# A gated linear attention block and an MLP on one core: the order of the turns is searched anew

## The chip, the core and the metric

The kernel runs on one core of a Trainium2 chip. A core has a matrix engine (TensorE, PE in the profile, its weight loads PEld), three engines for elementwise work (VectorE or DVE, ScalarE or ACT, GpSimd or POOL) and SyncE (SP), which here only issues DMAs. Each engine works through its own queue of instructions in the order in which the program wrote them, and waits on semaphores for the others. The metric is the device time of one launch in microseconds; lower is better.

## The reference, cut to what matters

There are 4 batches, 8 heads, 768 positions and a head width of 48. The first half is a recurrence over time, the second a layer norm and an MLP with a residual. All tokens are float32; the two weight matrices come as float64.

```python
for t in range(S):                      # state: B, H, 48, 48
    state = alpha[:, :, t, :, None] * state + einsum('bhd,bhe->bhde', k[:, :, t], v[:, :, t])
    y[:, :, t] = einsum('bhd,bhde->bhe', q[:, :, t], state)
x  = y, heads side by side              # B, 768, 384
xn = (x - mean(x)) / sqrt(var(x) + 1e-6) * g_ln
out = x + maximum(xn @ w_ch1, 0) @ w_ch2     # 384 -> 1536 -> 384
```

## The kernel before

**Tiles.** The 768 positions are cut into 6 chunks of 128. A tile is one chunk of one batch, so there are 24 tiles; tile "c b" is chunk c of batch b. `attention(c, b)` does one tile. It sums log alpha with a triangular matrix, scales q and k with the exponentials, forms the masked products inside the chunk, adds the part that the state of the chunk before brings, and brings the state forward. It then normalises the row and puts it, transposed, into `xT`.

**One tile is 23 turns**, each up to a `yield`: `la` (ACT, L246); `lps` (PE, L249); `ek`, `eq` (ACT, L253 and L254); `qk` for k (POOL, L256); `qk` for q (DVE, L258); loads for a later tile (SP); the first transposes `tps` (PE, L272) and their copy `qkT` (ACT, L276); the second ones and their copy (ACT in chunks 0 and 1, DVE at L278 later); `aps` (PE, L285); two masked copies `at` (DVE, L289); a DMA; `yps` (PE, L302 and L307); `x` (ACT, L311); a DMA; `sps` (PE, L321); `st` (DVE, two adds, L326); `st` times the gate (POOL, L331); `stats` (DVE L335 and L336, ACT L338 and L339); `xn` (DVE, L342); `xps` (PE, L349); `xT` (ACT, L351).

**The MLP.** Chunk 0 is plain: 12 blocks `hidden` (PE L372, then a relu on ACT) and `project` (PE L384, a DVE add). Chunks 1 to 5 use fast matrix multiplication with fewer products. The first layer has two rounds r of 15 products, `hidden_product` (PE L612), each followed by a combining step on DVE or ACT and, in places, on POOL (L620 to L655). Its operands are sums of `xT` that `combine_x` makes on DVE (L588). The second layer has 20 products, `product` (PE L455), followed by DVE, ACT or POOL steps (L465 to L515). Its operands are sums of the hidden block that `combine_hidden` makes on DVE (L442), after `relus` (ACT L664).

**Weights.** `take_weights(i)` turns one of 12 pieces of 768 KB from float64 into float32: three DVE steps (L168, L170, L172), one ACT step (L174), then DVE again (L176 and three times L183 for the first matrix, or L179 for the second), then the load of piece i + 3 into one of three staging buffers, of which the one that was freed first is taken.

**PSUM.** Three pools limit how far TensorE can run ahead: tag "a", 3 buffers, for `lps`, `tps` and `aps` (which takes 2); tag "s", 2 buffers, for `yps`, `sps` and `xps`; tag "m", 3 buffers, for the products of the MLP.

**The order.** All these generators are advanced one turn at a time by the string `ORDER` (L25 to L44), read by the two lines at L694 and L695. A small letter a to x is tile number 4c + b (a is tile 0 0, e is tile 1 0, x is tile 5 3). A to L are the 12 pieces of weights. M is the MLP, one half product per letter: a turn of matrix products, then its combining step. X is `combine_x`, N `combine_hidden`, R `relus`, S the sums of weights (POOL), O the reload of x for the residual. As the engines' queues keep the order of the program, the string fixes every queue. Positions in it are counted from 0 below.

Of the kernel before, what the change touches and what calls it, by code (L numbers as in the profile page):

```python
# [22 lines left out]


ORDER = (  # L25
    "babdabcdcabadcbacabbdabaabacababdabacbdbccbadAccdddcBcCedfeacbacaeBeffcgbaededbe"
    "eghfbAefgfcachfbdcheaaffbaefgdjBddeedbdcgfbeicCjgdfihcgjdCeAhccAgBDfghddEfeOgegi"
    "DfDeeiMfhMMMiMDMMiegMGEgEMMMOfeGghhigMMjhiCEfggFMhOGFHFgMGghMiHkfMMfiHeFIjhfHeMM"
    "IkJSIhhkhhlMMjIMfMglKJKjJLfgMljjLKLhhMSSMihSikMhOSgiMMSSMgShjkSjhiiMXjiSXSiXiXMk"
    "kMXkSllMXMXMlSMMXnMnMMkSMSMSiXmMSXMnMSMSMSMSjkMMkikjMXlMMMMMMRMllMMMljOMRSMMMSlk"  # L30
    "jlklMjjSRimMMnMSMjRMMMnMMMMkMnnmnMMMkMRMpjMMMnMRlMlllnmMmiRmOlMSmMRmMoMmmOMMJMRM"
    "SmSjmNSjlRMMRmoNinjkkNMmNMMkolMNRpoMlOKpMNMmMMMoMmoNmMNkNMMMNMMNMnMNqMkMNMMMopMM"
    "NSMMnolMoMlNpkNMoMMMOkOMMonnXXXXpMMXXMMXXXpoMMMMMMMMpXMMXMMoMMMrMMMMqMMMrMMMmnMM"
    "pRMomRnprmmMRqRopMMpMRMoMMmRmMMMMMrprnMnrnMMMoopppnMtpMqRMMMOMtrqMqnMMoMpqMprMRq"
    "RMMqNsMqMOMNRMNtrRnrMNMqMqqNMssRMMMNssoMMMNMNNMNsMMMNopMqqqqqrMMNMMsNtpMMNMMOprM"
    "MMNqsMqtMMooMMsNpMMXMMsMXXMstMqrrXtuXXXMtMMXXMMvMMMMXsvMMMtXMstMOrMMMMMMMMMvMMrr"
    "rsMtMvOsMMrtMMMMLuRMsMMvvMMMMMRRMtMrRMuMORvxMMMRRMstrMMstRqttsMqRuMsMMNRMuMRNMMN"
    "NMvMtuurvMxMMMMNsNtRtMMwNNvMMMsrMNMwMMNNMNMMwtNMMuMMuuMMMMMNuMwMNMMNwMMuttsxMMuv"
    "XXXvxMvuuXXXXxvwxMXMxxMMuwMXMwxMMXMMXMMMMMvMMwMwMxMMMRMuOwMuOMMwMMMMwuMMxwMwRMRM"
    "MxRMMRMvMMMMwxMMMMMMMMMuMMuMRMRRvMMMRNwxuRMMvMOMRxMMxvwMMNwMxNNMNxRNMMuxMMwMNMvM"  # L40
    "MONMwMNNMNMMMNwMMNMxMxMMvMMxwNMONMMNxMMMvMMXvOXXXMXXXMMMMMMXXMMMMMMMMXMMMMMRMXMM"
    "RMMMMMMMMMMMMMMMRRMMMMORMMMMMRMMMMRMMMMMMMMMRMRRMRMMNMMMNMMMNNNRMMNNMNMNMMMNNMMM"
    "ONMNMMMMMMMMMMMMMNNMMNMMMMMMM"
)  # L44


# [678 lines left out]
```

## Time and profile before

| | |
|---|---|
| Time, median of 3 | 476.33 us (474.06 to 476.4) |
| Span of the profiled execution | 472.3 us, granted clock 1.000 |
| PE, PEld busy | 457.1 us (97%), 384.5 us (81%) |
| DVE, POOL, ACT busy | 356.6 (76%), 222.7 (47%), 152.9 us (32%) |
| HBM read and written | 33.20 MB and 9.48 MB, 90 GB/s over the span |

The profile is one execution. Its busy times are sums over an engine's instructions, with overlaps counted once. A matmul's record lasts longer than the distance to the next one, since matmuls are pipelined, so how well TensorE is used is read from the distances between the starts of its records. An engine's idle time is put down to the instruction or DMA that ended it.

### The profile page before, as it was taken

To read this page: it belongs to the slowest core of one execution; us is meant where nothing else is said; L and a number is where in the kernel's file an instruction comes from. 1 tells how busy PE (TensorE), PEld (TensorE's weight loads), DVE (VectorE), ACT (ScalarE), POOL (GpSimd) and SP (SyncE) were. 2 spreads that over 40 slices of the span, in tenths; PEclk is the share of its full clock that TensorE was granted. 3 is DMA by queue.
4 is the path that set the end of the run, shared out by engine and by line. 5 is a ranking of instruction groups with operands and counts; after the bars stand their busy time and mean duration, and the time that the engine had idled before them with its cause. 6 is when DMAs were issued, how large, how long until landed. Compare 5 with 4: busy or idle time off the path is not lost.

```text
span 472.3 us, 9365 instructions
## 1 busy us (share of the span) xinstructions
PE 457.1 (97%) x3690; PEld 384.5 (81%) x3690; DVE 356.6 (76%) x662; ACT 152.9 (32%) x335; POOL 222.7 (47%) x222
## 2 busy tenths in 40 slices
PE   7899999999999999999999999999999999998996
PEld 5768465567688889998898998898998899987896
DVE  3799899867377799876788867688677579765673
ACT  4576354511033523124342121543031341223300
POOL 4142103069969990727461426460435360544513
PEclk9999999999999999999999999999999999999999
DMA  8986856403301422240331231330020110210001
GB/s 260 334 248 196 282 157 224 123 19 102 85 17 52 129 75 67 70 118 15 104 101 52 86 102 51 83 101 1 34 81 23 35 35 0 80 56 0 1 18 51
DMA packets 40132, 43.29 MB, mean 92 GB/s; under 512 B 13956, under 2 KB 36228, under 8 KB 40088
## 3 DMA queue, kind: packets, MB, share of 16 engines
q1 hardware_dynamic: 39544, 42.56, 29.4%
q8 instruction: 29, 0.48, 0.4%
q10 hardware_dynamic: 544, 0.13, 0.1%
q14 instruction: 15, 0.12, 0.1%
HBM read 33.20 MB, written 9.48 MB: 90 GB/s over the span
## 4 chain that ended last, share of the span: by engine, by line
PE 85%; DVE 5%; POOL 4%; ACT 2%; DMA 2%; issue 2%; POOLq 0%; DVEq 0%; ACTq 0%
PE ops L455 24%; PE hps L612 24%; PE hps L372 7%; PE ops L384 7%; PE aps L285 5%; PE yps L307 4%; PE tps L272 4%; PE yps L302 4%; PE lps L249 3%; PE sps L321 2%; PE xps L349 2%; DMA rk<-in_k_dram 1%; DVE at L289 1%; DVE sum L588 1%; DMA ra<-in_alpha_dram 1%
## 5 line engine op out<-in xcount | busy, mean ns | idle before, releaser
L471 POOL TENSOR_TENSOR ob<-ob,u 128x192 f32<-128x192 f32 x40 | 27.5, 699 | 83.3 <-DVE ob L468 63.9
L612 PE MATMUL hps<-sum,w 128*128 128x256 f32 x240 | 59.9, 382 | 1.1 <-DVE hT L655 1.1
L612 PEld LDWEIGHTS hps<-sum,w 128*128 128x128 f32 x240 | 44.7, 190 | 7.9 <-DVE hT L655 1.5
L455 PE MATMUL ops<-w,hT 128*128 128x192 f32 x280 | 49.6, 328 | 0.0
L664 ACT ACTIVATE hT<-hT 128x512 f32<-128x512 f32 x60 | 36.3, 628 | 35.6 <-POOL hT L634 21.3
L455 PEld LDWEIGHTS ops<-w,hT 128*128 128x128 f32 x280 | 45.7, 190 | 1.1
L331 POOL TENSOR_TENSOR st<-st,gate 128x384 f32<-128x384 f32 x20 | 19.1, 959 | 53.6 <-DVE st L326 44.3
L631 POOL TENSOR_TENSOR hT<-hT,u 128x512 f32<-128x512 f32 x10 | 12.9, 1287 | 56.9 <-DVE u L630 56.9
L256 POOL TENSOR_TENSOR qk<-rk,ek 128x384 f32<-128x384 f32 x22 | 23.3, 1059 | 30.0 <-PE sps L321 12.6
L307 PE MATMUL yps<-rv,at 128*64 128x48 f32 x768 | 36.5, 219 | 0.1
L289 DVE COPY_PREDICATED at<-consts,aps 128x512 f32<-128x512 int32 x48 | 32.2, 724 | 3.6 <-PE aps L285 3.2
L307 PEld LDWEIGHTS yps<-rv,at 128*64 128x64 f32 x768 | 32.9, 138 | 0.6 <-DVE at L289 0.3
L372 PE MATMUL hps<-xT,w 128*128 128x512 f32 x72 | 32.4, 597 | 0.0
L384 PE MATMUL ops<-w,hT 128*128 128x384 f32 x96 | 32.2, 488 | 0.0
L612 PE MATMUL hps<-xT,w 128*128 128x256 f32 x120 | 31.1, 382 | 0.9 <-DVE hT L644 0.9
L285 PE MATMUL aps<-qkT 48*128 48x128 f32 x384 | 28.6, 285 | 2.1 <-DVE at L289 1.3
L285 PEld LDWEIGHTS aps<-qkT 48*128 48x128 f32 x384 | 23.8, 187 | 8.0 <-issue 4.0
L302 PE MATMUL yps<-st,qkT 112*64 112x96 f32 x320 | 29.8, 257 | 0.0
L455 PE MATMUL ops<-ws,sum 128*128 128x192 f32 x160 | 28.9, 328 | 0.7 <-DVE sum L442 0.7
L455 PE MATMUL ops<-ws,hT 128*128 128x192 f32 x160 | 29.5, 327 | 0.0
L276 ACT COPY qkT<-tps 112x512 f32<-112x512 f32 x32 | 18.2, 597 | 29.0 <-PE tps L272 25.7
L455 PEld LDWEIGHTS ops<-ws,sum 128*128 128x128 f32 x160 | 26.3, 190 | 1.4 <-DVE sum L442 1.0
(141 smaller groups left out, 1020.9 us busy)
## 6 DMA issues: line engine op xcount, KB each, us to landing
ws<-in_moe_w_ch_dram SPq DMA_DIRECT2D x12, 768.0 KB, 6.1
ra<-in_alpha_dram SPq DMA_DIRECT2D x24, 192.0 KB, 2.6
rk<-in_k_dram SPq DMA_DIRECT2D x24, 192.0 KB, 3.4
rq<-in_q_dram SPq DMA_DIRECT2D x24, 192.0 KB
rv<-in_v_dram SPq DMA_DIRECT2D x24, 192.0 KB, 2.8
kept<-x SPq DMA_DIRECT2D x24, 192.0 KB, 1.9
ob<-kept SPq DMA_DIRECT2D x24, 192.0 KB, 2.9
out_dram<-ob SPq DMA_DIRECT2D x19, 192.0 KB, 1.9
```

Of the source, the lines that this page charges most:

```text
L256: nc.gpsimd.tensor_mul(qk[:, 1, :, :D], raws.pop(("k", c, b)), ek)
L285: nc.tensor.matmul(aps[i][:, p], qkT[rows, 1, p], qkT[rows, 0, p], start=True, stop=True)
L289: nc.vector.copy_predicated(out=at[:, i], data=aps[i], mask=mask.unsqueeze(1).broadcast_to([P, NP, P]))
L302: nc.tensor.matmul(yps[s, p].rearrange("p a b -> p (a b)"), qkT[:, 0, p, s], sts[b][:R, p].rearrange("p a b -> p (a b)"), start=True, stop ...
L307: nc.tensor.matmul(yps[s, p, i], at[:, i, p, s], vt[:, 2 * p + i], start=(c == 0), stop=(c == 0 or i == 1))
L331: nc.gpsimd.tensor_mul(st, st, gate.unsqueeze(2).broadcast_to([P, NP, 2 * D]))
L372: nc.tensor.matmul(hps, w1[:, f, j * P:(j + 1) * P], xT_of[c][:, f], start=(f == 0), stop=(f == NF - 1))
L384: nc.tensor.matmul(ops_of[b], hT_of[c][:, j, b], w2[:, j], start=(j == 0), stop=(j == NJ - 1))
L455: nc.tensor.matmul(acc, lhs[:, j], rhs[:, j], start=(j == 0), stop=(j == NT - 1))
L471: getattr(nc.gpsimd, f"tensor_{op}")(x, x, y)
L612: nc.tensor.matmul(acc[:, i], w, b, start=True, stop=True)
L664: nc.scalar.activation(out=x, in_=x, func=AFT.Relu)
```

## The change

The string `ORDER` is replaced by another one with the same letters in the same numbers, 1389 turns. So every instruction, every buffer and every operand stays; what changes is the sequence in which each engine's queue holds them, and with it the buffer that is taken where a pool has several. The new string begins with tile 0 0 and carries it, and then tile 0 2 and tile 0 1, several steps forward at once, where the old one brings all four batches forward side by side; tiles of chunk 1 (e to h) come in between those of chunk 0, from position 45 on (55 before). The purpose is a shorter wait of the engines for each other.

```diff
 ORDER = (
-    "babdabcdcabadcbacabbdabaabacababdabacbdbccbadAccdddcBcCedfeacbacaeBeffcgbaededbe"
-    "eghfbAefgfcachfbdcheaaffbaefgdjBddeedbdcgfbeicCjgdfihcgjdCeAhccAgBDfghddEfeOgegi"
-    "DfDeeiMfhMMMiMDMMiegMGEgEMMMOfeGghhigMMjhiCEfggFMhOGFHFgMGghMiHkfMMfiHeFIjhfHeMM"
-    "IkJSIhhkhhlMMjIMfMglKJKjJLfgMljjLKLhhMSSMihSikMhOSgiMMSSMgShjkSjhiiMXjiSXSiXiXMk"
...
-    "MxRMMRMvMMMMwxMMMMMMMMMuMMuMRMRRvMMMRNwxuRMMvMOMRxMMxvwMMNwMxNNMNxRNMMuxMMwMNMvM"
-    "MONMwMNNMNMMMNwMMNMxMxMMvMMxwNMONMMNxMMMvMMXvOXXXMXXXMMMMMMXXMMMMMMMMXMMMMMRMXMM"
-    "RMMMMMMMMMMMMMMMRRMMMMORMMMMMRMMMMRMMMMMMMMMRMRRMRMMNMMMNMMMNNNRMMNNMNMNMMMNNMMM"
-    "ONMNMMMMMMMMMMMMMNNMMNMMMMMMM"
+    "aacaaacbbcbacaaaaccccbbccaadabbbbbddbbddbaaaaeaacaccdddbbbbAgddebeeggeecaddcfccc"
+    "eeeeaaffbebccfihgedddddffghhiibdfdbbdgffcdfeejefACcfdAAcdggggeeeffBBeeggOghhBfMk"
+    "MMMiiOhjjChhhhDDOlMMMMCMMDCkFFDGBEGfggfjgEhhMMFFeEEffiijiiiMgkkGhhhhIIggkgiieMMM"
+    "MIjjeiIjjjigMSShHjjkmffSiSSMMMkhGJJJgigllMMkkjkMHjjjHjjkkiLLihHKSSSKKMlOMMMLllnn"
...
+    "RRMsMMMrNNNMMRMMMwwNNNMMMNNNMMtMMMMtrMMMNNNNOMMMsMNMMvMMtNsMMttMMMMNMMMxxuMMMMvv"
+    "vXXXXXXXXwwwuvvvuuuMMMMuuuXXXMMMuxxxMMMMMMMMMMMMMMMwwwwwMMMMMMMMMRwMMRRRMRMMOMwM"
...
+    "vMMMNwwMwMOMMMMMMNMNNNNMMwMMMMMMMwxxMMvwMXvvXXXXXXMMMMMMXXXMMXMMMMMMMMMMMMMMMMMM"
+    "MRMMMMMMMMMMMMMMMMMMMMMMMMMMMMMRMRRRRRROOMMMMRRMMMMMNRNNMMMNNOMMRMMNNNMMMLNMMMNN"
+    "MMOMMMNNMMMNNNMMMMMMMMMMMMMMM"
 )
```

More of the change, by code (lines that the diff above doesn't have):

```diff
@@ L25 @@
 ORDER = (
-    "babdabcdcabadcbacabbdabaabacababdabacbdbccbadAccdddcBcCedfeacbacaeBeffcgbaededbe"
-    "eghfbAefgfcachfbdcheaaffbaefgdjBddeedbdcgfbeicCjgdfihcgjdCeAhccAgBDfghddEfeOgegi"
-    "DfDeeiMfhMMMiMDMMiegMGEgEMMMOfeGghhigMMjhiCEfggFMhOGFHFgMGghMiHkfMMfiHeFIjhfHeMM"
-    "IkJSIhhkhhlMMjIMfMglKJKjJLfgMljjLKLhhMSSMihSikMhOSgiMMSSMgShjkSjhiiMXjiSXSiXiXMk"
-    "kMXkSllMXMXMlSMMXnMnMMkSMSMSiXmMSXMnMSMSMSMSjkMMkikjMXlMMMMMMRMllMMMljOMRSMMMSlk"
-    "jlklMjjSRimMMnMSMjRMMMnMMMMkMnnmnMMMkMRMpjMMMnMRlMlllnmMmiRmOlMSmMRmMoMmmOMMJMRM"
@@ L32 @@
[L32 to L37, printed above, removed]
@@ L38 @@
-    "NMvMtuurvMxMMMMNsNtRtMMwNNvMMMsrMNMwMMNNMNMMwtNMMuMMuuMMMMMNuMwMNMMNwMMuttsxMMuv"
-    "XXXvxMvuuXXXXxvwxMXMxxMMuwMXMwxMMXMMXMMMMMvMMwMwMxMMMRMuOwMuOMMwMMMMwuMMxwMwRMRM"
-    "MxRMMRMvMMMMwxMMMMMMMMMuMMuMRMRRvMMMRNwxuRMMvMOMRxMMxvwMMNwMxNNMNxRNMMuxMMwMNMvM"
-    "MONMwMNNMNMMMNwMMNMxMxMMvMMxwNMONMMNxMMMvMMXvOXXXMXXXMMMMMMXXMMMMMMMMXMMMMMRMXMM"
-    "RMMMMMMMMMMMMMMMRRMMMMORMMMMMRMMMMRMMMMMMMMMRMRRMRMMNMMMNMMMNNNRMMNNMNMNMMMNNMMM"
-    "ONMNMMMMMMMMMMMMMNNMMNMMMMMMM"
+    "aacaaacbbcbacaaaaccccbbccaadabbbbbddbbddbaaaaeaacaccdddbbbbAgddebeeggeecaddcfccc"
@@ new lines @@
+    "eeeeaaffbebccfihgedddddffghhiibdfdbbdgffcdfeejefACcfdAAcdggggeeeffBBeeggOghhBfMk"
+    "MMMiiOhjjChhhhDDOlMMMMCMMDCkFFDGBEGfggfjgEhhMMFFeEEffiijiiiMgkkGhhhhIIggkgiieMMM"
+    "MIjjeiIjjjigMSShHjjkmffSiSSMMMkhGJJJgigllMMkkjkMHjjjHjjkkiLLihHKSSSKKMlOMMMLllnn"
+    "nSSMMiiSSlhlhSSSSllffMhhXSSlMMiMMMllMMMnnMMMmllljkkjmXXXXlXXSXXSSSXXmmMMMllMMMMM"
+    "npmoSSMMMMMMMkknnjjMMMlMMMmmMMORRiRMMROmMmooMMMMiMMMMSSKMMSRSkkomkkMMMmMMMMMpMMn"
+    "nRjMMMMMpRRnnSmmMRmmmmMMMkMnNppprNnnnnMMMrrRNRRooMMMMpppOSooplNNNMMnMMoMMNNMMkNM"
@@ new lines @@
+    "MMNNNMMOMMMMoMMMMqMNMlmmmNNNMMMMoolMMMMMMMkMXXMXXXMXpXXXoooooMrrMMXXMMnMMMMpooqq"
+    "MMMMMMMMMMMMMOOOppppopqqqsMMMMMMMMMMqqqssRoMMMMMMrRRRRRMMMMMMRMrrMMpMMMqMMMOMrrq"
+    "qRRMMMMMNpqsRMMqqqqNNrNoMMqttrrRNtqMMMMnnNNssMtMmmMMMopuRNsnNNNpMMMqqMMMNttppMvM"
+    "sNMMMNNssJMMMMMMMNMMMMMMsnsXXsXXXrrrXXXXXXssssMMttsMMttMtrOtOMMMMMMMMrrtMMMMMvMM"
+    "MMMMMMuurrttttuMuuuMuuRRMMMMMMuMMMMMvvvvRRRMMMMMMMMMORMMMvMMxssMRMMMqqtvvRRMMMuu"
+    "RRMsMMMrNNNMMRMMMwwNNNMMMNNNMMtMMMMtrMMMNNNNOMMMsMNMMvMMtNsMMttMMMMNMMMxxuMMMMvv"
@@ L44 @@
+    "vXXXXXXXXwwwuvvvuuuMMMMuuuXXXMMMuxxxMMMMMMMMMMMMMMMwwwwwMMMMMMMMMRwMMRRRMRMMOMwM"
+    "MMMRxOwMMMxOxxMMMuMMuMMMRMMMMMRRMxxwxxxxxwwRRMMRMNMMNNxNxxMMMMMNMMMNNwMMxMNNNvvv"
+    "vMMMNwwMwMOMMMMMMNMNNNNMMwMMMMMMMwxxMMvwMXvvXXXXXXMMMMMMXXXMMXMMMMMMMMMMMMMMMMMM"
+    "MRMMMMMMMMMMMMMMMMMMMMMMMMMMMMMRMRRRRRROOMMMMRRMMMMMNRNNMMMNNOMMRMMNNNMMMLNMMMNN"
+    "MMOMMMNNMMMNNNMMMMMMMMMMMMMMM"
 )
```

## The prediction

> **What bounds the kernel now.** I read the busy times, then the distances between matmul starts, then stretches of 20 us, then the waits and the chain that ended last.
>
> ```profile
> PE 457.1 (97%) x3690; PEld 384.5 (81%) x3690; DVE 356.6 (76%) x662; ACT 152.9 (32%) x335; POOL 222.7 (47%) x222
> ```
>
> TensorE is busy nearly all the time; whether at full rate, pieces of the chain of waits tell (start, length, what):
>
> ```profile
> 263.80 2.60 PE ops L455 x16
> ...
> 276.16 1.09 PE aps L285 x16
> ...
> 279.57 4.32 PE hps L612 x20
> ```
>
> 16 records of L455 in 2.60 us are one every 162.5 ns, 20 of L612 in 4.32 us one every 216 ns, and in the whole trace this distance hardly varies. So each TensorE turn has a price, its start-to-start time where nothing waits: lps 0.645, four tps 0.437, aps 1.09, yps 1.74 (1.07 in chunk 0), sps 0.60 or 0.46 beside a yps or sps, xps 0.33, a hidden block 2.57, a project third 2.58, a hidden product 0.864, an output product 1.30 us. Each change from full 128x128 tiles to the smaller ones of aps, yps and sps costs 0.093 more (an aps alone between full tiles takes 1.184). The old order sums to 444.1 us. The first lps starts at 6.76 and the last record ends at 468.15, 461.4 later: TensorE is held up for 17.3 us, and 4 us of output follow. An order can win only from the hold-ups and the tile changes.
>
> ```profile
> core 0: us, PE busy (x) PEld busy (x) DVE busy (x) ACT busy (x) POOL busy (x), PEclk, DMA share, GB/s
> 20.00:40.00 20.00, 18.29 (x269) 14.06 (x268) 18.79 (x38) 14.70 (x34) 6.58 (x7) 1.00 0.78 219
> 40.00:60.00 20.00, 19.90 (x153) 11.83 (x150) 18.30 (x35) 10.38 (x23) 3.80 (x5) 1.00 0.86 272
> 60.00:80.00 20.00, 20.00 (x145) 11.05 (x143) 19.36 (x32) 9.21 (x17) 4.72 (x5) 1.00 0.55 172
> 80.00:100.00 20.00, 20.00 (x135) 12.35 (x135) 18.33 (x30) 9.31 (x19) 1.38 (x2) 1.00 0.36 110
> ```
>
> VectorE, 18.3 to 19.4 of 20 us, is the second bound here. Actual starts against summed prices place the hold-up: 7.6 us by 41 us, 5.0 from there to 400 us (0.82 at 254, 0.72 at 327, 0.36 at 167, the rest crumbs near 0.1), 4.7 in the last chunk. Where the first ends, VectorE's queue shows:
>
> ```profile
> 45.92 1.28 DVE L183 SCALAR_TENSOR_TENSOR w<-w,small,ws 128x256 f32<-128x256 f32 x3
> 47.11 0.56 DVE L258 TENSOR_TENSOR more<-rq,more 128x384 f32<-128x384 f32 x1
> 48.91 0.95 DVE L168 TENSOR_SCALAR w<-ws 128x768 int32<-128x768 int32 x1 [1.24 <-DMA ws<-in_moe_w_ch_dram]
> ```
>
> The first hidden block starts at 47.24, when these three L183 are done: VectorE set it. And the fourth piece of weights, issued at 41.94, lands at 48.9: 7.0 us; the fifth takes 6.1.
>
> The largest hold-up by one operand is near the end, in TensorE's order of time:
>
> ```profile
> 407.34 1.46 PE L455 MATMUL ops<-more,sum 128*128 128x192 f32 x8
> 408.64 0.49 PE L349 MATMUL xps<-consts,xn 128*128 128x128 f32 x3
> 408.96 1.47 PE L455 MATMUL ops<-w,sum 128*128 128x192 f32 x8
> 410.27 1.46 PE L455 MATMUL ops<-w,hT 128*128 128x192 f32 x8
> 411.57 1.03 PE L612 MATMUL hps<-xT,rq 128*128 128x256 f32 x4
> 413.69 1.13 PE L612 MATMUL hps<-sum,ra 128*128 128x256 f32 x4 [1.10 <-DVE sum L588]
> ```
>
> The last xps, then two output products and one hidden product (3.46 us); the next one waits for sums made from that xps.
>
> **What the Trainium skill says.** "TensorE: Matmul & The Clock Gate", section "Step-by-step: what each phase is for": matmuls stay in program order, only weight loads are pulled ahead. The trace agrees: what follows a waiting matmul waits too. "SBUF — State Buffer", section "Who interferes with whom": a VectorE instruction with two SBUF inputs contends with a GpSimd instruction that reads SBUF. The sums at L588 agree: 0.42 us alone, 0.70 while L471 runs. "Perfetto Trace Analysis", section "Identifying the Most-Contended Engine": matmul busy share doesn't measure headroom; hence the distances.
>
> **The change part by part.** Nothing is added or removed; each engine's sum of work stays. Four places differ.
>
> *Tile changes.* Writing out TensorE's queue from each string, I count 34 entries into small tiles before and 28 after: 6 x 0.093 = 0.56 us less. 14 of 20 sps lie beside a yps or sps before, 16 after: 2 x 0.136 = 0.27. No work hides this. **-0.8 us.**
>
> *The start.* I follow the new queues with durations from the trace. lps 0 0 at 6.76 is seen by ACT at 8.28, as its like is before. Its ek and eq, la 0 1 and the exponentials of 0 2 and 0 1 follow; the last eq ends at 11.4. It frees the PSUM buffer for tps of 0 2 (11.45), whose copy ends at 12.85 and frees the one for aps 0 0: 12.9 (13.95 before). VectorE masks that at 14.2 to 15.55; buffers freed so let in tps 0 1 (15.0), its copy (to 16.3), aps 0 1 (16.4), masked from 17.7. aps 0 2 runs at 19.1, la 1 0 at 20.3 when alpha has landed (before, k of that tile landed at 21.2), lps 1 0 at 22.65, aps 0 3 at 25.45, aps 1 0 at 29.0. TensorE has 18.7 us of turns ahead of it: hold-up 29.0 - 6.76 - 18.7 = 3.5 us, against 6.8 before after as much work. That looks like a gain of 3.3, but VectorE has postponed its weights. From the end of aps 1 0 to yps 1 3 (turns 89 to 225) TensorE has 37.1 us: 7 hidden blocks 18.0, 4 yps 6.3, 8 tps 3.5, 3 aps 3.3, the rest 6. yps 1 3 needs the PSUM buffer that st 1 1 frees, and from at 1 0 to st 1 1 VectorE has, at its distances between starts: 6 times L168, L170, L172 at 2.25, 6 endings of a piece at 2.18, 4 pairs of at at 1.29, 4 qk at 0.60, 4 xn at 0.42, 3 pairs of st at 0.71, 2 stats at 0.72: 39.35 us. With 0.3 of latency TensorE comes 2.55 us late, or 0.5 if every VectorE step has its smallest distance. The same sum before, from aps 0 0 to the first hidden block, is 30.8 against 27.4, so 3.7 late, on a hold-up of 2.9 at aps 0 0; with 1 us of VectorE idle it makes the 7.6. So sums at these prices are trusted.
> The new order also adds a wait. Turns 182 to 193 hold, on VectorE, the endings of pieces 2 and 3, then at once the starts of 5, 6 and 4. Piece 6 goes into the buffer that the ending of piece 2 frees and is needed 2.18 + 2.25 = 4.4 us later, piece 4 similarly; loads took 6.1 and 7.0. Queued behind are at 1 3, st 1 1 and the copy for aps 2 0, for which TensorE waits. Bounds: 0.5 us if the loads take 4.5 to 5 (an estimate from 768 KB at 272 GB/s, 2.8, and the 1.9 from issue to landing of a small DMA on the page), 3.6 if they take 7 and queue for each other. I take 1.5, as the attention loads come earlier now. New hold-up: 3.5 + 2.55 + 1.5 = 7.55. **0 us**, from -3.1 (3.5 + 0.5 + 0.5) to +3.
>
> *Chunks 1 to 4.* The three old waits for VectorE (0.82, 0.72, 0.36) belong to places that no longer exist: -1.9. New ones: at the begin of chunk 4 (turns 1039 to 1076) a masked pair, 11 sums, two qk, stats, xn and two combining steps stand between aps 5 1 and what lets hidden product 1 start (the PSUM buffer of product 5): 10.3 us of VectorE against 8.7 of TensorE, with sums at 0.5 each: 2.0 late with latency, 0.7 with the smallest distances. I take 1.3. At turn 854 the copy for aps 4 3 lies behind 11 sums: 8.4 against 7.8, late by 0 to 0.8; I take 0.4. Chains over several engines I can't read off; for them 0.5, a third of what the old order shows. The POOL chain of a hidden round (7 steps of 1.26 us from combining 9) keeps 0.6 us or more of other TensorE work in hand in chunks 1 to 4, so costs nothing. **+0.3 us**, -1.2 to +3.
>
> *The end.* The last xps (5 1) now stands after the output product that it preceded: 2.16 us of TensorE work cover the sums instead of 3.46. One add of output leaves the sums' way (0.3), and POOL, which slows them, ends sooner by the shift (0.25). **+0.75 us** (0.5 to 1.0). The hidden rounds of chunk 5 have no other work in either order, and the last products the same output chain: 0.
>
> Sum: -0.8 + 0 + 0.3 + 0.75 = +0.25; 476.33 becomes 476.6.
>
> **The rivals.** *Faster:* VectorE keeps to its small distances and the loads come in 5 us. Start -3.1, chunks -1.2, end +0.5, tiles -0.8: -4.6, 471.7. For it: ACT and TensorE are ahead in the start, POOL is light until 100 us (1.4 to 6.6 of 20 us). Against: the old start fits the full distances. *Slower by the loads:* hold-up 4.5 at aps 1 0 (a walk by hand leaves out small waits), full lateness, wait 3.6: 10.65, so +3; chunks 2.0 + 0.8 + 0.5 - 1.9 = +1.4, end +0.75, tiles -0.8: +4.35, 480.7. For it: DMA share 0.86 at 40 to 60 us. Against: loads for tiles are through earlier. *Slower in the chunks:* start as forecast, but chains over ACT, POOL and VectorE bring 3.3 us instead of 0.5: +3.05, 479.4. For it: the new string groups letters, so VectorE's queue has bursts. Against: POOL's chains have slack.
>
> **How the numbers follow.** Forecast (within 0.5%, 2.4 us) 0.48; faster rival 0.27; slower by loads 0.15; slower in the chunks 0.10. The range, 471.5 to 481.0, takes in both outer cases and leaves a bit under 2 in 10 out. Faster by over 0.5% 0.27, same 0.48, slower 0.25.
>
> **What would show it.** Right: aps 1 0 near 29 us; hold-up under 4 us then and 7 to 8 by 85; idle VectorE before L168 until a DMA of weights, 1 to 2 us in all; hidden product 3 of chunk 5 held up by 1.8 to 2.2; entries into small tiles 28. Wrong: VectorE done with piece 4 before TensorE needs at 1 3; a wait at another chunk's begin over 1 us; or TensorE short of work before aps 1 0, when alpha of chunk 1 lands after 21 us.

## The result and the profile after

The new order takes 483.81 us (median of four, 482.86 to 484.26), the old one beside it 476.37 us: ratio 1.016, 95% interval 1.0135 to 1.0185. It is slower by 7.4 us, above the forecast of 476.6 and above the range. The profiled execution of after is the longest of its four (span 482.5 us) and that of before the shortest (472.3), so the two traces differ by 10.2 us, not 7.4; sizes read from them are told with that in mind. Six of the 27 executions of before beside e5 to e8, and one of 15 beside e16 and e17, took 481 to 485 us at a lower granted clock; distances in us leave them out, and the ratios of e5 to e7, with wide intervals, come out lower than these distances.

The page's first part, after: busy time of each engine, its share of the span and its number of instructions.

```profile
PE 459.9 (95%) x3690; PEld 385.7 (80%) x3690; DVE 353.2 (73%) x662; ACT 154.7 (32%) x335; POOL 224.9 (47%) x222
```

The same instructions, and about the same busy times. The page's fourth part, the chain that ended last, is what changed. First before, then after:

```profile
PE 85%; DVE 5%; POOL 4%; ACT 2%; DMA 2%; issue 2%; POOLq 0%; DVEq 0%; ACTq 0%
```

```profile
PE 67%; DVE 20%; POOL 4%; DMA 4%; ACT 2%; issue 2%; SPq 0%; POOLq 0%; DVEq 0%; ACTq 0%
```

VectorE carries a fifth of the chain instead of a twentieth. Where, the stretches of 20 us tell; after, the four that answer to those shown of before, and the next:

```profile
20.00:40.00 20.00, 17.43 (x260) 13.29 (x258) 15.71 (x30) 13.65 (x36) 6.51 (x7) 0.91 0.86 244
40.00:60.00 20.00, 19.25 (x147) 11.42 (x146) 19.50 (x31) 11.36 (x22) 3.46 (x3) 1.00 0.60 176
60.00:80.00 20.00, 16.16 (x149) 9.82 (x148) 17.50 (x29) 5.79 (x9) 3.42 (x3) 0.83 0.46 148
80.00:100.00 20.00, 19.99 (x173) 12.58 (x170) 18.94 (x29) 6.19 (x14) 15.30 (x14) 1.00 0.57 180
100.00:120.00 20.00, 18.68 (x143) 11.94 (x142) 16.62 (x23) 7.86 (x14) 8.18 (x10) 1.00 0.28 99
```

and of before the stretch that was not shown:

```profile
100.00:120.00 20.00, 20.00 (x139) 13.19 (x138) 11.47 (x19) 2.55 (x5) 20.00 (x27) 1.00 0.23 75
```

The fourth column is VectorE. Between 20 and 40 us it works 15.7 us instead of 18.8, and 5 us of its work have moved beyond 100 us. The piece of weights that is ready last is ready at 119.4 us instead of 97.9. The column before the DMA share is the granted clock: 0.91 and 0.83 in two stretches, 1.00 everywhere before.

TensorE's hold-up by place (actual starts against summed prices, as in the prediction): before, 8.3 us up to the first hidden product of chunk 1, 4.4 in chunks 1 to 4 and 4.7 in chunk 5. After: 18.4, 5.3 and 4.9. The loss is in the start. These sums count every slower matmul as hold-up too. The first large wait, from the chain of after (start, length, what):

```profile
28.48 4.19 DMA ra<-in_alpha_dram
32.67 0.02 issue
32.69 0.94 ACT la L246 x2
33.64 0.04 issue
33.68 2.93 PE lps L249 x4
```

ScalarE's queue holds the logarithm of tile 2 0 (position 94) ahead of that of tile 1 3 (95) and of the copy of tile 0 3. The alpha of tile 2 0 lands at 32.7 us, so all three wait, TensorE for lps 1 3, and then VectorE. VectorE's part, in its order of time (the bracket: idle time before and what ended it):

```profile
34.72 0.45 DVE L342 TENSOR_SCALAR xn<-x,mv,rstd 128x384 f32<-128x384 f32 x1
38.59 0.48 DVE L342 TENSOR_SCALAR xn<-x,mv,rstd 128x384 f32<-128x384 f32 x1 [3.42 <-ACT rstd L339]
...
46.79 1.81 DVE L170 SCALAR_TENSOR_TENSOR w<-ws,w 128x768 f32<-128x768 uint32 x1
48.63 1.25 DVE L172 TENSOR_SCALAR ws<-ws 128x768 int32<-128x768 int32 x1
...
69.14 0.95 DVE L168 TENSOR_SCALAR w<-ws 128x768 int32<-128x768 int32 x1 [2.11 <-DMA ws<-in_moe_w_ch_dram]
70.13 0.96 DVE L170 SCALAR_TENSOR_TENSOR w<-ws,w 128x768 f32<-128x768 uint32 x1
71.12 0.56 DVE L172 TENSOR_SCALAR ws<-ws 128x768 int32<-128x768 int32 x1
71.59 1.34 DVE L289 COPY_PREDICATED at<-consts,aps 128x512 f32<-128x512 int32 x2
```

Three things are to be seen: 3.42 us of idle time from the late alpha; 2.11 us of waiting for the weights of piece 4, with `at` 1 3 queued behind, as the prediction said; and the same two rounding steps (L170 and L172) at 1.81 and 1.25 us at 46.8 but 0.96 and 0.56 at 70. POOL's rows show what lies beside the long ones:

```profile
46.79 1.00 POOL L256 TENSOR_TENSOR more<-rk,ek 128x384 f32<-128x384 f32 x1
47.74 1.72 POOL L256 TENSOR_TENSOR qk<-rk,ek 128x384 f32<-128x384 f32 x1
```

TensorE meets VectorE's lateness here:

```profile
65.69 2.84 PE L372 MATMUL hps<-xT,w 128*128 128x512 f32 x6
72.38 1.96 PE L272 MATMUL tps<-consts,qk 128*112 128x128 f32 x8 [3.84 <-DVE at L289]
74.12 4.63 PE L372 MATMUL hps<-xT,w 128*128 128x512 f32 x6
```

It stands for 3.8 us, and the hidden block behind the pause takes 4.6 us instead of 2.8: half rate, the 0.83 of the table.

### The profile page after: what moved, and what is told of

It reads as the page before. It is cut to its first block, busy times and chain, and to the rows that moved or that the text cites. A ratio compares the mean times of both kernels' runs of the same rounds, so it can differ in the third digit from the quotient of the medians.

```text
span 482.5 us, 9373 instructions
## 1 busy us (share of the span) xinstructions
PE 459.9 (95%) x3690; PEld 385.7 (80%) x3690; DVE 353.2 (73%) x662; ACT 154.7 (32%) x335; POOL 224.9 (47%) x222
## 4 chain that ended last, share of the span: by engine, by line
PE 67%; DVE 20%; POOL 4%; DMA 4%; ACT 2%; issue 2%; SPq 0%; POOLq 0%; DVEq 0%; ACTq 0%
PE hps L612 24%; PE ops L455 23%; PE ops L384 4%; PE aps L285 3%; PE tps L272 3%; PE lps L249 2%; PE yps L307 2%; DVE at L289 2%; DVE w L170 2%; DVE ws L176 2%; PE yps L302 2%; DVE w L183 2%; DMA ra<-in_alpha_dram 2%; DVE w L168 2%; DMA ws<-in_moe_w_ch_dram 1%
## 5 line engine op out<-in xcount | busy, mean ns | idle before, releaser
L471 POOL TENSOR_TENSOR ob<-ob,u 128x192 f32<-128x192 f32 x40 | 26.3, 668 | 93.5 <-DVE ob L468 72.7
L331 POOL TENSOR_TENSOR st<-st,gate 128x384 f32<-128x384 f32 x20 | 17.9, 894 | 62.0 <-DVE st L326 23.8
L256 POOL TENSOR_TENSOR qk<-rk,ek 128x384 f32<-128x384 f32 x22 | 26.5, 1209 | 30.3 <-issue 16.9
L372 PE MATMUL hps<-xT,w 128*128 128x512 f32 x72 | 34.4, 627 | 0.2 <-DVE w L183 0.2
L465 DVE TENSOR_TENSOR ob<-ops,ob 128x192 f32<-128x192 f32 x50 | 17.6, 353 | 19.7 <-POOL ob L471 9.2
L272 PE MATMUL tps<-consts,qk 128*112 128x128 f32 x176 | 26.2, 283 | 5.6 <-DVE at L289 4.4
L272 PEld LDWEIGHTS tps<-consts,qk 128*112 128x112 f32 x176 | 21.0, 139 | 12.7 <-DVE at L289 4.7
```

Source lines behind the costliest of these rows:

```text
L256: nc.gpsimd.tensor_mul(qk[:, 1, :, :D], raws.pop(("k", c, b)), ek)
L272: nc.tensor.transpose(tps[:, p], qk_of(c, b)[:, i, p].rearrange("p a b -> p (a b)")[:, :R], ident)
L372: nc.tensor.matmul(hps, w1[:, f, j * P:(j + 1) * P], xT_of[c][:, f], start=(f == 0), stop=(f == NF - 1))
L471: getattr(nc.gpsimd, f"tensor_{op}")(x, x, y)
```

## Experiments

Seventeen kernels. "After" and "before" are the two orders; the ratio and the distance are always to before, run beside it. Its median moves between 475.4 and 476.4 us from group to group, so gains are read from distances: after stands 7.4 us above before.

**Where the loss sits: the orders crossed (e1, e2).** Turns 0 to 339, all up to the first hidden product of chunk 1, come from the old order and the rest from the new one, each letter's turns kept in number.

```diff
-    "aacaaacbbcbacaaaaccccbbccaadabbbbbddbbddbaaaaeaacaccdddbbbbAgddebeeggeecaddcfccc"
+    "babdabcdcabadcbacabbdabaabacababdabacbdbccbadAccdddcBcCedfeacbacaeBeffcgbaededbe"
...
-    "nSSMMiiSSlhlhSSSSllffMhhXSSlMMiMMMllMMMnnMMMmllljkkjmXXXXlXXSXXSSSXXmmMMMllMMMMM"
+    "kMXkSllMXMXMlSMMXnMnmkjkjjjjjkkniillSSSllSSlillnnMMmllljkkjmlSXSSSXXmmMMMllMMMMM"
```

> The first 340 turns are those of the order before (all up to the first hidden product of chunk 1); the rest keeps the new order. Theory (the loss lies in the start): hold-up at the first hidden product of chunk 1 about 8 us as before, so 476 to 478 us. Rival (the loss lies in the chunks and the end): still over 481 us.

479.11 us, ratio 1.0086 (1.0039 to 1.0132).

The counterpart has the new order's turns 0 to 361, again all up to that product, and then the old one's (the diff is against after):

```diff
-    "nSSMMiiSSlhlhSSSSllffMhhXSSlMMiMMMllMMMnnMMMmllljkkjmXXXXlXXSXXSSSXXmmMMMllMMMMM"
-    "npmoSSMMMMMMMkknnjjMMMlMMMmmMMORRiRMMROmMmooMMMMiMMMMSSKMMSRSkkomkkMMMmMMMMMpMMn"
+    "nSSMMiiSSlhlhSSSSllffMhhXSSlMMiMMMllMMMnnMXXXXXXXMMMMXMXMMMSMSMSMMMXMMMMMMRMMMMO"
+    "MRSMMMSkkMSRmMMMSMjRMMMMMMMkMnnmnMMMkMRMpjMMMnMRlMlllnmMmiRmOlMSmMRmMoMmmOMMJMRM"
...
```

> The first 362 turns are those of the new order; the rest keeps the order before. Theory (start): 482 to 484 us, with 16 to 18 us of hold-up by the first hidden product of chunk 1. Rival (chunks and end): 476 to 478 us.

486.13 us, ratio 1.0212 (1.0179 to 1.0246). With the old start the hold-up before chunk 1 is 11.7 us, with the new one 15.7; each seam makes waits of its own (in e1 1.8 us at aps 2 3, in e2 5 us more in chunk 1 than before has), so 2.8 and 9.8 us don't add up to 7.4. The start is the larger part; a seam costs too much for a finer split.

**The logarithm (e3).** Turn 94 moved behind lps 1 3.

```diff
-    "eeeeaaffbebccfihgedddddffghhiibdfdbbdgffcdfeejefACcfdAAcdggggeeeffBBeeggOghhBfMk"
+    "eeeeaaffbebccfhgedddddffghhiiibdfdbbdgffcdfeejefACcfdAAcdggggeeeffBBeeggOghhBfMk"
```

> New order, one turn moved: the logarithm of tile 2 0 (turn 94) now stands just before the matmul of its sums (turn 108), behind four steps of ACT on tiles of chunks 0 and 1. Theory A (ACT's queue stands still for the alpha of tile 2 0, and all behind it with it): no wait of 2.2 us before the lps of tile 1 3, no half-rate matmuls there, VectorE's 3.4 us of idle before 38.6 gone; 3 to 5 us less than the new order, 479 to 481 us. Rival B (VectorE's amount of work sets the hold-up at the first chunk-2 tile anyway): the gain is given back by 80 us, 483 to 484 us.

481.43 us, ratio 1.0113 (1.0087 to 1.0139): 5.1 us above before instead of 7.4, so about 2.3 us won, less than theory A's 3 to 5. In its trace VectorE's wait for rstd is 1.71 us, not 3.42, and the wait for the weights of piece 4 is gone in that execution. Fewer things stand behind the alpha of tile 2 0.

**The place of piece 4 (e4).** Its four turns stand further back; pieces 5 and 6 keep theirs.

```diff
-    "MMMiiOhjjChhhhDDOlMMMMCMMDCkFFDGBEGfggfjgEhhMMFFeEEffiijiiiMgkkGhhhhIIggkgiieMMM"
+    "MMMiiOhjjChhhhDDOlMMMMCMMDCkFFDGBGfggfjghhMMFFeffiEEijiiiMgkkGEEhhhhIIggkgiieMMM"
```

> New order, four turns moved: VectorE's start of weight piece 4 and its ACT step go from turns 193 and 201 to before turn 214, its ending and the next load from 209 and 210 to before turn 224. So the masks of tile 1 3 no longer stand behind a start that waits for its load. Theory A (the wait for the load and the burst of three starts hold up the masks, and the pause halves TensorE's rate after it): the pause of 3.8 us before the tps of tile 2 0 gone, 5 to 7 us less, 477 to 479 us. Rival B (amount of VectorE's work): only the 2.1 us of waiting saved at most, 482 us.

482.42 us, ratio 1.014 (1.0108 to 1.0173): theory B's time, and a gain of some 1.3 us that lies within the intervals. The pause ahead of tps 2 0 is gone, and VectorE waits for no load of weights in this trace. In its place have come 1.4 us of idle time at aps 2 0 (behind ScalarE's step of piece 4, which waited for VectorE) and 2.0 at tps 2 1 (for `at`, VectorE again); yps 1 3 then ran at half rate, about 1 us longer. Without the load in the way VectorE is still late, only elsewhere.

**The clock (e5).** Useless matmuls in the two pauses, called by two new turns of the string.

```diff
+    def fill():
+        for count in (3, 5):
+            t = ps.tile([P, 512], FP32, name="hps", tag="m", bufs=3)
+            for _ in range(count):
+                nc.tensor.matmul(t[:, :2 * P], tri, consts, start=True, stop=True)
+                nc.tensor.matmul(t[:, 2 * P:], tri, consts, start=True, stop=True)
+            yield
```

> The order of after, with useless matmuls (their result is never read) put into TensorE's queue at the two places where it stands idle in the start: six of 256 columns, 2.6 us, ahead of lps 1 3 and ten, 4.3 us, ahead of the first tps of tile 2 0. Theory A (part of the loss is TensorE at half rate for some us after each of the two pauses, about 4.6 us in the profiled execution of after): the pauses are filled, the turns behind them run at their full rate, the hold-up that shows beside lps 1 3 .. tps 1 1 and in the hidden blocks behind tps 2 0 is gone; time 2 to 4 us less than after, 480 to 482 us. Theory B (what comes out of the pause waits for VectorE and ACT anyway, so a slow TensorE costs nothing): no less time than after, 483 to 486 us, the waits come back at the next places.

482.73 us, ratio 1.012 (1.0047 to 1.0194). The rows behind the second pause, now filled:

```profile
71.63 1.04 PE L272 MATMUL tps<-consts,qk 128*112 128x128 f32 x8
72.50 2.74 PE L372 MATMUL hps<-xT,w 128*128 128x512 f32 x6
```

1.04 and 2.74 us where after has 1.96 and 4.63, and the granted clock is 1.00 all through: without the pause there is no half rate. The time is 1.1 us below that of after, but 7.3 us above before, hardly less than after's 7.4, and its executions (481.82 to 484.19 us) overlap with those of after. So what the half rate costs is at most about 1 us and not clear of the spread; theory A's 2 to 4 us are not there.

**POOL's sums later (e6).**

```diff
-    "MIjjeiIjjjigMSShHjjkmffSiSSMMMkhGJJJgigllMMkkjkMHjjjHjjkkiLLihHKSSSKKMlOMMMLllnn"
+    "MIjjeiIjjjigMhHjjkmffiMMMkhGJJJgigllMMkkjkMHjjjHjjkkiLLihHKKKMlOMMMLllnnSSSSSSSS"
```

> The order of after, with POOL's first eight sums of weights (turns 253 to 306) put behind turn 319, nothing else. Theory A (VectorE is the bound of the start and its rounding steps are stretched by POOL's work at the same time): the five or so L179 that lie between 86 and 105 us fall from 1.6 to about 1.0 us each, VectorE is done 2 to 3 us earlier there, the wait of 1.25 us at aps 2 2 shrinks; time 1 to 3 us less than after, 481 to 483 us. Theory B (hold-up there comes from the weights' loads or from TensorE itself): L179 falls but the time stays within 0.7 us of after; and if hidden product 11 or 3 of chunk 1 then waits for POOL's sums, it is 1 us more.

487.78 us, ratio 1.0224 (1.0147 to 1.0301), 12 us above before. L179 falls from 1.46 to 1.13 us on average before 106 us, but hidden products 3, 5 and 10 of chunk 1 now wait 2.3, 0.8 and 0.8 us for those sums. Theory B, and worse than it had it: nothing won before chunk 1 (16.0 us of hold-up; e2, same turns there, 15.7).

**POOL's k left out in chunks 0 and 1 (e7).**

```diff
-        nc.scalar.activation(out=ek, in_=lv, func=AFT.Exp, scale=-1.0)
+        nc.scalar.activation(out=ek if c > 1 else qk[:, 1, :, :D], in_=lv, func=AFT.Exp, scale=-1.0)
...
-        nc.gpsimd.tensor_mul(qk[:, 1, :, :D], raws.pop(("k", c, b)), ek)
+        k = raws.pop(("k", c, b))
+        if c > 1:
+            nc.gpsimd.tensor_mul(qk[:, 1, :, :D], k, ek)
```

> The order of after; in chunks 0 and 1 k is left out (the exponential is written straight into the scaled k, so the eight POOL multiplications at L256 are gone; everything else is the same work). Theory A (POOL's multiplications stretch VectorE's rounding steps at L170 and L172): up to the second copy of tile 2 1 VectorE's busy time falls from 72 us to 66 to 69, L170 is 1.0 and L172 0.56 again where L256 stood beside them, and the hold-up before chunk 1 (18.4 us in after) falls by 3 to 6 us; time 477 to 481 us. Theory B (the loads of weights and alpha make the pauses, VectorE only waits for them): the busy time falls, the waits for DMA grow by as much, time 482 to 484 us.

482.62 us, ratio 1.0115 (1.0029 to 1.0201), 7.2 us above before. VectorE's busy time to the second copy of tile 2 1 falls from 72.4 to 68.5 us, about as theory A said, but VectorE idles more in the first 40 us (18.8 us instead of 14.3: the alpha of tile 2 0 held lps 1 3 up for 3.5 us in this execution), and the time is theory B's. Up to there two L170 or L172 stayed long, and beside them stand the multiplications of chunk 2, which this kernel keeps; one of them (POOL's row, its line number two higher in this kernel, then VectorE's):

```profile
65.48 1.78 POOL L258 TENSOR_TENSOR qk<-rk,ek 128x384 f32<-128x384 f32 x1 [16.35 <-DVE w L168]
```

```profile
65.45 0.96 DVE L170 SCALAR_TENSOR_TENSOR w<-ws,w 128x768 f32<-128x768 uint32 x1
66.44 1.25 DVE L172 TENSOR_SCALAR ws<-ws 128x768 int32<-128x768 int32 x1
```

**Both moves (e9).** The diffs of e3 and e4 together; as in e4, only piece 4 moves, though the expectation names pieces 5 and 6 as well.

> The order of after with the two moves of the third and fourth run together: the logarithm of tile 2 0 behind lps 1 3, and the starts of pieces 5, 6 and 4 further back. Theory A (two causes of their own, the wait for alpha and the wait for weights): the gains add, 2.4 and 1.4 us, 479.5 to 480.5 us. Theory B (behind both stands VectorE's amount of work up to 118 us, so removing the second wait only hands over to it): 481 to 482 us, no better than the first move alone.

481.09 us, ratio 1.0135 (1.0102 to 1.0168), 5.6 us above before: no better than e3 alone. Theory B.

**Less work for VectorE, in both orders (e10, e11).** This is the run that tells who sets the start.

```diff
-        stt(out=dst, in0=lo.bitcast(UINT32), scalar=2.0 ** -32, in1=dst.bitcast(INT32),
-            op0=AOP.mult, op1=AOP.add)
```

> The order of after; the step at L170 is left out, so the low words of the weights are not added: VectorE has 12 x 0.99 = 11.9 us less to do, all of it between 22 and 118 us. Theory A (VectorE's amount of work sets the start of the new order): the hold-up before chunk 1 falls from 18.4 us (15.7 in another execution) to 8 to 11 us, time 475 to 478 us, and the distance to the order of before with the same step left out is at most 3.5 us. Theory B (loads of alpha and weights and the queue of ACT set it): hold-up 13 to 16 us, time 480 to 483 us, distance to before at least 5 us.

476.15 us, ratio 1.0014 (0.9995 to 1.0032); hold-up before chunk 1 10.5 us.

> The order of before; the step at L170 is left out, as in the run for after. 7.3 of its 8.3 us of hold-up before chunk 1 come before 36 us, where VectorE has only three of these steps, so little is to be won. Theory A and B alike: 472.5 to 476 us; what is compared is the distance to the run for after.

476.47 us, ratio 1.0008 (0.9986 to 1.0029). Of the 11.9 us less the new order turns about 7 into time (its distance to before falls from 7.4 to 0.6 us) and the old one none; the distance between the orders goes from 7.4 us to nothing that can be measured. The chain of the new order without that step:

```profile
PE 79%; DVE 7%; DMA 6%; POOL 4%; ACT 1%; issue 1%; SPq 1%; POOLq 0%; DVEq 0%; ACTq 0%
```

VectorE's 20% have become 7%, although the waits for alpha and for weights are all still in this trace (3.0 us at lps 1 3; 2.3 and 0.9 us before two L168). With less work for VectorE the new order is as fast as the old one, with these late loads in it.

**Idle time filled (e13, e14).** A rounding step that is ready, put ahead of the normalisation that waits; e14 has e3's move as well.

```diff
-    "eeeeaaffbebccfihgedddddffghhiibdfdbbdgffcdfeejefACcfdAAcdggggeeeffBBeeggOghhBfMk"
+    "eeeeaaffbebccfihgedddddffghhiibdfdbbdgffcCdfeejefAcfdAAcdggggeeeffBBeeggOghhBfMk"
```

> The order of after; one turn moved: the start of piece 2 (L168, L170, L172, 2.3 us of VectorE) stands ahead of xn 0 3 instead of eight turns behind it, into the time in which VectorE waited 3.42 us for rstd. Theory A (idle time of VectorE before 40 us is work that is missing later, until 118 us): all later VectorE steps come 2.0 to 2.3 us earlier, time 481.3 to 482.3 us. Theory B (only the stretching of the steps and the loads count): the waits for loads grow by as much, time 483 to 485 us.

481.72 us (479.85 to 483.06), ratio 1.0117 (1.0083 to 1.0151). The median is theory A's, the executions spread over both theories, and the profiled one doesn't show the mechanism: alpha landed late again (3.5 us at lps 1 3), and VectorE, done with the rounding, then idled 2.1 us before `at` 1 1. Not conclusive alone.

> The order of after with the logarithm of tile 2 0 behind lps 1 3 (third run, 481.4 us) and the start of piece 2 ahead of xn 0 3 (thirteenth). Theory A (VectorE's idle time counts, from whatever cause): the third run still had 1.9 us of VectorE's idle time between 30 and 40 us more than before has; filling half of it gives 0.5 to 1.5 us, 480 to 481 us. Theory B (nothing left to fill that matters): 481 to 482 us.

480.89 us, ratio 1.0115 (1.0088 to 1.0143). Here the gap is filled:

```profile
33.95 0.45 DVE L342 TENSOR_SCALAR xn<-x,mv,rstd 128x384 f32<-128x384 f32 x1
34.32 0.95 DVE L168 TENSOR_SCALAR w<-ws 128x768 int32<-128x768 int32 x1
35.30 0.96 DVE L170 SCALAR_TENSOR_TENSOR w<-ws,w 128x768 f32<-128x768 uint32 x1
36.29 0.56 DVE L172 TENSOR_SCALAR ws<-ws 128x768 int32<-128x768 int32 x1
36.77 0.98 DVE L342 TENSOR_SCALAR xn<-x,mv,rstd 128x384 f32<-128x384 f32 x1
```

By 40 us VectorE has idled 11.5 us, in before 11.3. The time lies in theory A's range, but 5.5 us of distance are left, no less than the 5.1 of e3, so the filled gap itself has won nothing that shows. The idle time is worth about 2 us, all of it won by e3.

**Stretched steps, with the gap filled (e16, e17).** e14 with e7's edit, now for chunks 0 to 2, and before with the same edit.

> The order of the fourteenth run; in chunks 0 to 2 k is left out (the exponential goes straight into the scaled k, so twelve POOL multiplications at L256 are gone). Theory A (what is left of the loss in the start is VectorE's steps stretched beside POOL): VectorE's stretch by 80 us falls from 6.4 to about 2 us, hold-up before chunk 1 from 14.8 to 10.5 to 12 us, time 477 to 478.5 us against 480.9. Theory B (something else, such as the loads of weights or the order of the turns themselves): the stretch falls, idle time takes its place, time 479.5 to 481.5 us.

478.84 us, ratio 1.0057 (1.0037 to 1.0077); stretch of VectorE's steps by 80 us about 0.3 us, hold-up before chunk 1 12.8.

> The order of before with the same POOL work left out. There the stretch by 80 us is 2.2 us, nearly all of it in the first three scalings of q, and VectorE is not what bounds after 41 us. Theory A: little is won, 474.5 to 476.4 us, so that the distance between the orders shrinks from 5.5 (fourteenth run) to 1.5 to 3.5 us. Theory B: the distance stays at 4 us or more.

476.02 us, ratio 1.0012 (0.9991 to 1.0033). The distance falls from 5.5 to 2.8 us: POOL's multiplications cost about 2.5 us in the new order and nothing measurable in the old. Theory A in kind, short of it in size. The edit also takes POOL's step out of each tile's own chain; that the gain comes from the stretched steps and not from this is argued, not shown. 2.8 us stay; the waits left in e16's start are 1.6 us at lps 2 0 (logarithm), and 1.0, 1.7 and 1.3 us at tps 2 0, yps 1 3 and aps 2 2, all three for VectorE.

**A better order, from the start (e12).** The first 76 turns of after, then the old order's, with e8's tail.

```diff
-    "babdabcdcabadcbacabbdabaabacababdabacbdbccbadAccdddcBcCedfeacbacaeBeffcgbaededbe"
+    "aacaaacbbcbacaaaaccccbbccaadabbbbbddbbddbaaaaeaacaccdddbbbbAgddebeeggeecaddcBCfB"
...
```

> The first 76 turns of the order of after (its forwarded first tiles), then the turns that are left in the order of before, with the last tile's transposes earlier as in the eighth run. Theory A (the forwarded start is a gain of its own, 3.6 us less hold-up at aps 1 0, and is lost only by what comes behind it): 471.5 to 474 us, faster than both kernels. Theory B (VectorE's work up to the first hidden block decides, and the forwarded start only moves the wait): 474.5 to 477 us.

478.44 us, ratio 1.007 (1.0046 to 1.0095): slower than both theories. The old turns behind the new ones wait 3.8 us at lps 1 3 and 2.3 at lps 1 0. In this mix the forwarded start brings nothing that lasts; its seam makes waits of its own, as in e1 and e2, so it is no test of the forwarded start alone.

**A better order, from the end (e8, e15).** The old order; xps 5 1 and its copy stand two output products earlier, and two sums come forward.

```diff
-    "MONMwMNNMNMMMNwMMNMxMxMMvMMxwNMONMMNxMMMvMMXvOXXXMXXXMMMMMMXXMMMMMMMMXMMMMMRMXMM"
+    "MONMwMNNMNMMMNwMMNMxMxMMvMMxwNMONMMNxvMvMMXXMMOXXMXXXMMMMMMXXMMMMMMMMXMMMMMRMXMM"
```

> The order of before; only the last tile's transposes (xps 5 1) stand two output products earlier, its copy right behind, and the first two sums of chunk 5 before the output of product 13. Theory A (hidden product 3 of chunk 5 is held up by 1.26 us because the sums made from that xps come late, 3.46 us of TensorE work ahead): with 6 us of work ahead the hold-up is below 0.3 us and the time 0.8 to 1.3 us less than before, 475 us. Theory B (the sums are late because VectorE has the outputs of chunk 4 to do anyway): hold-up stays over 0.9 us and the time within 0.4 us of before.

475.55 us, ratio 0.9984 (0.9964 to 1.0003). Hidden product 3 still waits 0.96 us: the sums stand on VectorE behind outputs that wait for TensorE. The wait is theory B's; the time, about 0.8 us less by the ratio, has an interval that takes in no change. So the sums were moved further:

```diff
-    "MONMwMNNMNMMMNwMMNMxMxMMvMMxwNMONMMNxMMMvMMXvOXXXMXXXMMMMMMXXMMMMMMMMXMMMMMRMXMM"
+    "MONMwMNNMNMMMNwMMNMxMxMMvMMxwNMONMMNxvMvXXMMXXMMOXXXMMMMMMMXXMMMMMMMMXMMMMMRMXMM"
```

> The order of before with the last tile's transposes two products earlier, as in the eighth run, and its sums no longer behind the outputs of products 17, 13 and 7 on VectorE: two ahead of the first, two ahead of the second, three ahead of the third. Theory A (in the eighth run the sums waited behind outputs that wait for TensorE, so only 0.3 of the 1.26 us came back): the wait of hidden product 3 of chunk 5 falls below 0.4 us, time 0.9 to 1.3 us less than before, ratio about 0.9977. Theory B (another wait takes its place, hidden product 11 or the next ones for PSUM): ratio 0.999 to 1.001.

473.55 us against 475.38 of before, ratio 0.9975 (0.9956 to 0.9994): about 1.2 us less than before by the ratio, theory A, and so faster than both orders. Hidden products 11 and 3 of chunk 5 now follow each other, 0.87 us apart; the 0.16 us that remain at the one after are small change:

```profile
411.51 1.03 PE L612 MATMUL hps<-xT,rq 128*128 128x256 f32 x4
412.38 1.03 PE L612 MATMUL hps<-sum,ra 128*128 128x256 f32 x4
413.40 1.13 PE L612 MATMUL hps<-sum,w 128*128 128x256 f32 x4
```

## Why the prediction was wrong

| Step, as the prediction put it | Forecast | Measured (profiled) |
|---|---|---|
| Entries into small tiles | 34 to 28, -0.8 us | as counted, at the same prices |
| aps 1 0: start, hold-up | 29.0, 3.5 us | 28.77, 3.5 us |
| VectorE, at 1 0 to st 1 1 | 39.35 us and 1.5 of waiting for loads | 48.33 us |
| Hold-up at yps 1 3 | 7.55 us | 15.9 us |
| From there to chunk 1 | nothing new | 2.5 us |
| Chunks 1 to 4 | +0.3 us | 5.3 - 4.4 = +0.9 us |
| Hidden product 3 of chunk 5 | 1.8 to 2.2 us | 1.73 us |
| The end in all | +0.75 us | 4.9 - 4.7 = +0.2 us |

The step that failed is **"The start: 0 us"**, in the part that takes VectorE's 39.35 us against TensorE's 37.1. The walk to aps 1 0 was right, and the mechanism, VectorE late up to yps 1 3, was right too. Its size was not. The 68 VectorE steps at the distances taken do sum to 39.35 us; 48.33 were measured, because 5.99 us of idle time and 2.99 us of longer steps come on top. VectorE freed the buffer for yps 1 3 at 78.29 us, and nearly all of the 15.9 us is its lateness; in this execution TensorE, at half rate, came to yps 1 3 at 79.13, while in e16 it stands there for 1.6 us. Of the idle time, 2.11 us is the wait for weights (forecast 1.5, bounds 0.5 to 3.6), but 3.42 us is the wait for rstd, behind the alpha of tile 2 0. The prediction named "when alpha of chunk 1 lands after 21 us" among what would make it wrong; it was alpha of chunk 2, which a walk that ended at aps 1 0 never came to. Of the 2.99 us, 2.2 are three steps stretched beside POOL (L170 at 46.79, L172 at 48.63 and at 65.79). They were left out because the distances were taken from the old order, in which no L170 and no L172 is stretched (959 and 585 ns at most). The other 0.8 is a wrong mean: the 2.25 us for L168, L170 and L172 is an average over all 12 pieces, 2.45 for the six of the first matrix and 2.05 for those of the second, and five of the six starts in this stretch are of the first. Count, busy time and mean in ns over all pieces, first before, then after:

```profile
L170 DVE SCALAR_TENSOR_TENSOR w<-ws,w 128x768 f32<-128x768 uint32 x12 | 11.5, 958 | 0.4
L172 DVE TENSOR_SCALAR ws<-ws 128x768 int32<-128x768 int32 x12 | 6.8, 564 | 0.4
```

```profile
L170 DVE SCALAR_TENSOR_TENSOR w<-ws,w 128x768 f32<-128x768 uint32 x12 | 13.5, 1127 | 0.4
L172 DVE TENSOR_SCALAR ws<-ws 128x768 int32<-128x768 int32 x12 | 8.9, 744 | 0.4
```

The Trainium skill, "SBUF — State Buffer", section "Who interferes with whom", was cited for the sums at L588 alone; it says the same of VectorE instructions with two SBUF inputs and of `tensor_scalar` where it takes two ports, which fits L170 (two inputs) and L172. The trace agrees: 0.96 to 1.81 and 0.56 to 1.25 us. Asking it of every VectorE operation that moves beside POOL would have pointed to the term.

A second error of the same step: it stopped at yps 1 3. "That VectorE has postponed its weights" holds until the last piece, at 119.4 us, and 2.5 us more of hold-up come until then. A term nobody wrote down is the half rate behind the pauses, at most about 1 us by e5.

In chunks 1 to 4 the sum came near by luck. Neither of the two waits that the prediction priced came: hidden product 1 of chunk 4 (1.3 us) and aps 4 3 (0.4) start with less than 0.1 us of hold-up. Others came: 1.35 us at hidden product 3 of chunk 2, for VectorE's sums, which is the "wait at another chunk's begin over 1 us" of the prediction's list, 1.1 at tps 5 0 for VectorE's scaled q, and 0.7 at output product 12 of chunk 2.

Of the rivals, "slower by the loads" had the direction and not the cause: e4 and e9 show that taking the wait for weights away wins some 1.3 us alone, within the intervals, and nothing on top of e3. What e10 and e11 show is a rival that was missing: VectorE is the bound of the new start, so what makes it idle or slow, from any engine, is paid for. From the runs, of the 7.4 us: some 2 for the late alpha in front of the other logarithms (e3, e14), some 2.5 for POOL's multiplications (e16, e17), each uncertain by more than 1 us. The rest, near 3, wasn't separated; weights put late in VectorE's queue and the small waits of chunks and end are candidates. What the half rate costs may be contained in these shares.

The claim that the last tile's place costs 0.75 us held for its wait (1.73 against 1.26), but the wait of hidden product 12 in chunk 5 became shorter by 0.26, so the end as a whole came to +0.2. e15 turns the same reading round and wins about 1.2 us on the old order.

## What to carry to other kernels

Before reordering queues, write down for the engine that is second in load how much of its work is done by each point of time: here the order that let it idle early paid for it later. Durations from a trace belong to the neighbours that they had in that trace, and a mean over a line's instructions may mix two kinds; where a reorder puts a VectorE step beside POOL work on SBUF, price it from both sides. Follow a hand walk of the queues until the bound engine has caught up, not only to the first place that looks better, and ask for each load how many turns stand behind the one that waits for it.

## What was not expected of the hardware

After pauses of 2.2 and 3.8 us TensorE ran at half rate for some microseconds (a hidden block in 4.57 us, start to start, instead of 2.57); with the pauses filled by useless matmuls it did not. The Trainium skill, "TensorE: Matmul & The Clock Gate", section "What's actually happening", says so: after an idle window of about 3.4 us the clock is halved until it has been busy as long again, and the window doesn't start with the kernel. The length of a pause alone doesn't decide here: half rate followed pauses of 1.73 us in e3 and 2.02 in e4, below the page's figure, and none followed one of 3.06 us in e14. A window that runs on its own fits. In after, where the fourth figure is the granted clock:

```profile
33.55:36.96 3.41, 3.28 (x7) 0.50 0.78 231
36.97:71.09 34.12, 30.82 (x296) 1.00 0.60 183
71.11:77.92 6.81, 5.54 (x13) 0.50 0.22 71
```

The half rate lasts 3.41 us and twice that, and its two stretches begin 37.55 us apart, 11 times 3.41, though the pauses before them begin 37.1 us apart. The clock also differs between executions of one and the same kernel: before took 474.0 us at a mean granted clock of 1.000, 475.4 at 0.995 and 476.4 at 0.993, but also 472.8 at 0.999, so it isn't all that differs.

L168 takes 0.55 or 0.95 us for the same shape with POOL idle in both cases (after, 64.21 us, piece 6, and 69.14 us, piece 4). In both orders the six pieces of the first matrix take 0.94 to 0.95 us and those of the second 0.53 to 0.56 (one 0.74, with POOL at work beside it). What differs in the program is the destination: three separate runs of 256 columns in the first matrix, one of 768 in the second. That this is the reason, no run here tests.
